# State products ahead of score sums, and weight conversion regrouped, in a fused recurrent-attention and two-stage MoE kernel

## The chip, the cores and the metric

One core of one Trainium2 chip runs the whole program. The metric is device time in microseconds (us) of one execution; the kernel before has a median of 840.31 us over 3 runs (839.7 to 840.45). Five engines work side by side, each through its own queue in program order, and wait for one another through semaphores: TensorE (PE, matmuls), VectorE (DVE), ScalarE (ACT), GpSimd (POOL) and SyncE (SP, which here issues the DMAs).

## The reference

```python
for t in range(S):                          # B, H, S, D = 4, 8, 768, 48
    kt, vt, rt = (k[:, :, t], v[:, :, t], r[:, :, t])
    cur = np.einsum('bhd,bhe->bhde', u[None] * kt, vt)
    y[:, :, t] = np.einsum('bhd,bhde->bhe', rt, state + cur)
    state = w[None, :, :, None] * state + np.einsum('bhd,bhe->bhde', kt, vt)
...
h = x @ w_in                                # 3072 tokens, 384 -> 2048; weights in float64
g = np.maximum(h, 0.0) + alpha * np.minimum(h, 0.0)
x = (g @ w_out).astype(np.float32)          # 2048 -> 384
...
logits = x @ w_gate                         # 8 experts, 384 tokens each, best logits first
h = np.maximum(x[mask] @ w1[e], 0.0)        # 384 -> 1024
out[mask] = h @ w2[e]                       # 1024 -> 384
```

Three stages follow one another: a recurrence over 768 positions with a 48x48 state for each of 32 heads, a leaky-ReLU MLP over all 3072 tokens, and a routed MLP in which each token goes to one expert.

## The kernel before, in words

The recurrence is computed in chunks of 128 positions: 24 chunks, in the order chunk-major over 4 batch entries. `turn(i)` (L353) works on chunk i and finishes chunk i-1; it is a generator of four sections, and the loop at L1271 runs turns 0 to 24. Within a turn PE gets, in this order: the products of the scaled receptance with the stored state into y (L371, only from the second chunk of a batch entry on), four transposes of a later chunk's keys into pk (L339), the score sums of chunk i+1 (`sums`, L308: 16 tiny matmuls of prod with uw into the last eight columns of the tile kvc), the state products kv of chunk i (L390, into the first columns of the same tile kvc, not in the last four turns that have a chunk), the products of V with the masked scores AT of chunk i-1 into y (L397), and the scores pA of chunk i (L424). DVE copies pA into AT by predicate at the start of the next turn (L366), scales the receptance (RT, L331), copies the sums to cs (L318) and adds kv to the state (Sn, L402). ACT writes the scaled diagonals of AT (L378, L405), copies pk to KT (L345) and y to ysb (L410). POOL scales keys (L324), decays the state (SW, L382) and multiplies RT by KT into prod (L351), which the sums of the next turn read. SP loads the chunks and stores ysb.

Between the sections of a turn runs a second generator, the weight preparation (`load_weights`, L462). The MLP multiplies in pairs of a high and a low part, so each of 32 pieces of its weights (16 of `w_in`, 16 of `w_out`, 128x384 each, in float64) is loaded three pieces ahead and converted in five steps (`weight_split`, L438). Steps 1 to 4 each have one DVE instruction (L449, L451, L453 into ti; L456 into tf), step 1 also the load of a later piece and mk on ACT (L446); step 5 is the cast of the high part on ACT (L459) and the subtraction for the low part on POOL (L460). `PACE` = 4 of these steps are taken in each turn from turn 2 on; after the loop a piece that has been begun is finished, and four warm-up matmuls follow (L1278 to L1280). That makes 19 pieces in this stage.

Then `mlp` (L575) takes the tokens in groups of 512, five of them, and two of 256. It splits the group's x into xh and xl (L512, L513), and for each of 16 steps f it does nine matmuls of layer 1 into ph (L656), reads ph twice on ACT (nt L660, gt L661), combines the two on DVE (gt, L669), casts to gh on ACT (L677) and subtracts for gl on DVE (L680). Layer 2 of step f (12 matmuls, L605) is issued two steps later. Each step also takes `rate` steps of a side generator (L678): in group 0 five steps of the weight preparation (13 pieces remain), in groups 1 and 2 the gate columns (L517), which read the gate table wgb. That table is loaded when group 1 begins (L624), into a pool opened where the pool of mk and tf was closed. Groups 3 and 4 have early logits there. The constants for routing, `route_consts` (L116), among them two zeroed tables ohr of 128x3072 bf16, are made on POOL and DVE right after the first x is split (L593).

Of the kernel before, what the change touches and what calls it, by code (L numbers as in the profile page):

```python
# [8 lines left out]
F32 = mybir.dt.float32  # L9
# [13 lines left out]
NTT = NT // P  # L23
# [4 lines left out]
GMAX = max(GROUPS)  # L28
WCG = 3
WO = DM + E  # L30
PACE = 4
BITS = (5, 5, 5, 5, 4, 4, 4)
STEPS = 4
TH = 32
# [25 lines left out]
def cut(g, n):  # L60
    for _ in range(n):
        if next(g, "end") == "end":
            return
        yield
# [21 lines left out]
class Kernel:  # L86
# [29 lines left out]
    def route_consts(self):  # L116
        nc, cp = self.nc, self.cp
        v, g = nc.vector, nc.gpsimd
        self.tri = cp.tile([P, P], BF, name="tri")
        v.tensor_scalar(self.tri, self.jp, 0.0, -1.0, op0=ALU.is_le, op1=ALU.mult)  # L120
        self.onesb = cp.tile([P, P], BF, name="onesb")
        g.memset(self.onesb, 1.0)
        self.ones48 = cp.tile([P, 2 * NTT], F32, name="ones48")
        g.memset(self.ones48, 1.0)
        io = cp.tile([P, P], F32, name="io")
        g.iota(io, pattern=[[1, P]], base=0, channel_multiplier=0, allow_small_or_imprecise_dtypes=True)
        self.io = io
        ii = cp.tile([P, NSL + TH], I32, name="ii")
        g.iota(ii[:, :NSL], pattern=[[1, NSL]], base=BASE32, channel_multiplier=0)
        g.iota(ii[:, NSL:], pattern=[[1, TH]], base=0, channel_multiplier=0)  # L130
        self.iob, self.ioa = ii[:, :NSL], ii[:, NSL:]
        self.io1 = cp.tile([P, TH], F32, name="io1")
        v.tensor_scalar(self.io1, io[:, :TH], 1.0, None, op0=ALU.add)
        self.pcol = cp.tile([P, 1], F32, name="pcol")
        g.iota(self.pcol, pattern=[[0, 1]], base=0, channel_multiplier=1, allow_small_or_imprecise_dtypes=True)
        self.ohr = []
        for i in range(2):
            t = self.rp.tile([P, NTT, 4, 32], BF, name=f"ohr{i}")
            g.memset(t, 0.0)
            self.ohr.append(t)  # L140
        S = self.S = self.ps.tile([P, 512], F32, name="S")
        self.kap, self.act, self.sel = S[:, 0:24], S[:, 24:48], S[:, 48:56]
        self.bad, self.esum, self.tau, self.u = S[:, 56:57], S[:, 57:58], S[:, 58:59], S[:, 64:88]
        self.xi, self.bi5, self.ai5 = (S[:, 96 + 24 * i:120 + 24 * i].bitcast(I32) for i in range(3))
        self.iot = S[:, 168:192]
        v.memset(S[:, 56:58], 0.0)
        v.memset(self.act, 1.0)
        v.tensor_copy(self.iot, io[:, :NTT])
# [156 lines left out]
            t = self.raw[n, i % NRAW[n]]  # L305
            self.nc.sync.dma_start(t.rearrange("p j t -> p (j t)") if n == "r" else t, src[c, b])

    def sums(self, i):  # L308
        if i >= NCH:
            return  # L310
        cc, prod = self.kvc[:, 4 * D:], self.prod.pop(i)
        for j in range(4):
            for c in range(2):
                o = slice(64 * c, 64 * c + 64)
                self.nc.tensor.matmul(cc[o, 2 * j:2 * j + 2], prod[:, j, o], self.uw[:, j, :], start=True, stop=True,
                                      skip_group_check=True)
        cs = self.cs[i] = self.wk.tile([P, H], F32, name="cs")
        self.nc.vector.tensor_copy(cs, cc)  # L318

    def scale_k(self, i, g=None):  # L320
        if i >= NCH:
# [31 lines left out]
    def turn(self, i):  # L353
# [26 lines left out]
        self.scale_r(i + LOOK)  # L380
        if prev and pc < NCB - 1:
            g.tensor_mul(self.SW[pb], self.Sn[(i - 1) % 2], self.WC)  # L382
        yield
        self.sums(i + 1)
        kv = None
        if cur and c < NCB - 1:
            kv = self.kvc[:112, :4 * D].rearrange("p (j d) -> p j d", j=4)
            for j in range(4):
                for q, m in enumerate((64, D)):
                    nc.tensor.matmul(kv[64 * q:64 * q + m, j, :], KP[:, 2 * j + q, :m], head(V, 2 * j + q, D),  # L390
                                     start=True, stop=True, skip_group_check=True)
        if prev:
            Vp, ATp = self.raw["v", (i - 1) % NRAW["v"]], self.AT.pop(i - 1)
            for j in range(4):
                for q in range(2):
                    m = 112 - 64 if q else 64
                    nc.tensor.matmul(y[64 * q:64 * q + m, j, :], head(Vp, 2 * j + q, m), ATp[:, q, j, :],  # L397
                                     start=(pc == 0), stop=True, skip_group_check=True)
        if kv is not None:
            for q in range(2):  # L400
                o = slice(64 * q, 64 * q + D)
                v.tensor_add(self.Sn[i % 2][o, :, o], kv[o], self.SW[b][o, :, o])  # L402
        if cur:
            for h in range(1, H, 2):
                nc.scalar.mul(AT[:, 1, h // 2, :], self.ident, cs[:, h:h + 1])  # L405
# [169 lines left out]
    def mlp(self, ctx):  # L575
# [11 lines left out]
        c0 = ExitStack()  # L587
        self.stg = self.pool(c0, "stg2", 2)
        side = self.wl
        rate = 5  # L590
        todo = []
        drain(self.split_x(0))
        self.route_consts()  # L593
        acc = pend = None

        def layer2(gi, f, gh, gl, tiles=None):
# [22 lines left out]
        for gi, T in enumerate(GROUPS):  # L619
# [23 lines left out]
            xh, xl = self.x  # L643
            nx = self.split_x(gi + 1) if gi < late else iter(())
            for f in range(NF):
                if f == 4 and gi < late:
                    self.fetch_x(gi + 1)
                if f > 9:
# [10 lines left out]
                gt = self.gp.tile([P, GMAX], F32, name="gt" if gi < late else "gh", bufs=2 if gi < late else 3)  # L659
                nc.scalar.activation(nt[:, :T], ph[:, :T], AF.Relu, scale=-1.0)  # L660
                nc.scalar.activation(gt[:, :T], ph[:, :T], AF.Relu)  # L661
                if len(todo) == (LAG if gi < late else LAG + 1):
                    j = todo.pop(0)
                    if j[0] < late:
                        assert self.split_done > NF + j[1]
                        layer2(*j)
                    else:
                        self.late_gate(lg, j)
# [580 lines left out]
def kernel(ctx, tc, *args):  # L1249
# [5 lines left out]
    with ExitStack() as c2:  # L1255
        K.pa = c2.enter_context(tc.tile_pool(name="pa", bufs=1, space=PSUM))
        K.rw = ctx.enter_context(tc.tile_pool(name="rw", bufs=4, reuse_waits="tile"))
        wl = K.wl = K.load_weights(WAHEAD)
        K.att_setup(c2)
        v = tc.nc.vector  # L1260
        for i in range(LOOK + 1):
            K.scale_k(i, None if i else v)
        for i in range(LOOK):
            K.scale_r(i)
            K.turn_k(i)
            K.keep_k(i)
            K.product(i, None if i else v)
        K.sums(0)
        for i in range(EARLYC, AHEAD):
            K.load_chunk(i)  # L1270
        for i in range(NCH + 1):  # L1271
            merge((K.turn(i), 1), (cut(wl, PACE) if i > 1 else None, 1))
            K.load_chunk(i + AHEAD)
            if 17 <= i < 20:
                K.fetch_x(0, (i - 17,))
            if i == 3:
                tc.nc.sync.dma_start(K.al, K.alpha.rearrange("(f p) -> p f", p=P))
        while K.splitting:  # L1278
            next(wl)
        K.warm(4)  # L1280
    K.pa = None
    tc.nc.vector.tensor_scalar(K.al, K.al, -1.0, None, op0=ALU.mult)
    K.mlp_pools(ctx)
# [46 lines left out]
```

## Time and profile before

| | |
|---|---|
| median of 3 runs | 840.31 us |
| profiled execution | 834.65 us, its span 832.9 us |
| busy, share of the span | PE 94%, DVE 69%, ACT 49%, POOL 34% |
| granted TensorE clock, mean | 0.98 |
| chain that ended last | PE 69%, DVE 15%, issue 6%, ACT 4% |
| bytes moved | 81.39 MB, mean 98 GB/s |

The page divides the span into 40 slices of 20.8 us. The attention loop fills the first seven, group 0 of the MLP the next three and a half; from there to slice 26 PE is busy in nine tenths or more of each slice. Busy shares say where an engine has no time left, and the chain says which engine's work was waited for; a PE share under nine tenths in a slice is where PE itself waited. Times in the rows below are counted from the span's start.

### The profile page before, as it was taken

The page shows a single profiled execution, that of the slowest core. Times are in us where ns is not written, and L with a number is a line of the kernel's source. Part 1 is how long each engine was busy: PE and PEld are TensorE (multiplying, and loading weights), DVE is VectorE, ACT ScalarE, POOL GpSimd, SP SyncE. Part 2 cuts the span into 40 slices and gives each one's busy share as a digit, 9 for nine tenths or more (in the row PEclk, how much of TensorE's full clock was granted, in tenths as well). Part 3 has the DMA queues.
Part 4 walks back from the last instruction along what each step waited for, and adds up shares of the span by engine and source line. Part 5 has one row for each costly group of instructions (what it writes and reads, how often), then busy time and mean ns, then how long its engine had stood idle before and what let it go on. Part 6 is the DMA issues. An engine that isn't in the chain of part 4 may idle for free.

```text
span 832.9 us, 16734 instructions
## 1 busy us (share of the span) xinstructions
PE 785.5 (94%) x6147; PEld 717.9 (86%) x6147; DVE 576.9 (69%) x1536; ACT 406.7 (49%) x875; POOL 280.2 (34%) x269
## 2 busy tenths in 40 slices
PE   7888889899999999999999999996999999999996
PEld 6677778687899999999999999986899999999996
DVE  5688888878789989988988434565766666664121
ACT  2777778455544444444444445542443443444341
POOL 5676774421000000000000000003476666668661
PEclk8799999999999999999999999998899999999999
DMA  6577785241220020021020001006434633635400
GB/s 196 171 215 209 210 237 149 86 131 39 77 76 1 0 77 1 10 96 30 19 70 27 1 26 33 20 1 197 155 92 147 209 102 109 202 111 173 142 30 31
DMA packets 64585, 81.39 MB, mean 98 GB/s; under 512 B 8048, under 2 KB 55408, under 8 KB 64368
## 3 DMA queue, kind: packets, MB, share of 16 engines
q1 hardware_dynamic: 61008, 70.81, 27.5%
q0 software_dynamic: 3072, 9.44, 3.3%
q8 instruction: 50, 0.82, 0.4%
q14 instruction: 39, 0.32, 0.1%
q10 hardware_dynamic: 416, 0.00, 0.0%
HBM read 66.07 MB, written 14.16 MB: 96 GB/s over the span
## 4 chain that ended last, share of the span: by engine, by line
PE 69%; DVE 15%; issue 6%; ACT 4%; POOL 2%; DMA 1%; DVEq 0%; POOLq 0%; SPq 0%; ACTq 0%
PE m L605 21%; PE ph L656 19%; PE eph L1106 10%; PE o L1123 9%; PE cnt L796 2%; DVE AT L366 2%; DVE ti L451 2%; DVE ti L449 2%; PE y L397 2%; PE kvc L390 1%; DVE ti L453 1%; DVE tf L456 1%; PE pA L424 1%; DVE RT L331 1%; ACT nt L660 1%
## 5 line engine op out<-in xcount | busy, mean ns | idle before, releaser
L605 PE MATMUL m<-wbh,gl 128*128 128x384 f32 (+1 forms) x352 | 120.4, 342 | 5.6 <-DVE gl L680 5.6
L656 PE MATMUL ph<-xh,wah 128*128 128x512 f32 (+1 forms) x336 | 122.7, 365 | 2.0 <-ACT xh L512 1.8
L656 PE MATMUL ph<-xl,wah 128*128 128x512 f32 (+1 forms) x336 | 122.7, 365 | 0.4 <-DVE xl L513 0.4
L656 PE MATMUL ph<-xh,wal 128*128 128x512 f32 (+1 forms) x336 | 122.5, 365 | 0.0
L605 PE MATMUL m<-wbh,gh 128*128 128x384 f32 (+1 forms) x352 | 119.5, 339 | 0.0
L605 PE MATMUL m<-wbl,gh 128*128 128x384 f32 (+1 forms) x352 | 119.3, 339 | 0.0
L660 ACT ACTIVATE nt<-ph 128x512 f32<-128x512 f32 (+1 forms) x112 | 60.1, 536 | 112.7 <-PE ph L656 106.8
L746 POOL COPY L<-M 128x176 f32<-128x176 f32 (+1 forms) x2 | 0.7, 356 | 339.0 <-DVE M L611 318.0
L669 DVE SCALAR_TENSOR_TENSOR gt<-nt,al,gt 128x512 f32<-128x512 f32 (+1 forms) x96 | 67.8, 706 | 52.7 <-ACT gt L661 52.7
L677 ACT CAST gh<-gt 128x512 fp32r<-128x512 f32 (+1 forms) x96 | 56.4, 587 | 75.5 <-DVE gt L669 75.5
L1114 DVE SCALAR_TENSOR_TENSOR hl<-eph,hh 128x384 fp32r<-128x384 f32 x64 | 35.6, 557 | 77.4 <-ACT hh L1109 77.4
L1109 ACT ACTIVATE hh<-eph 128x384 fp32r<-128x384 f32 x64 | 31.4, 491 | 114.6 <-PE eph L1106 110.1
L605 PEld LDWEIGHTS m<-wbh,gl 128*128 128x128 f32 x352 | 66.1, 188 | 9.8 <-DVE gl L680 9.8
L527 DVE SCALAR_TENSOR_TENSOR junk<-wt,wgb 128x384 f32<-128x384 f32 x128 | 71.3, 557 | 3.9
L656 PEld LDWEIGHTS ph<-xh,wal 128*128 128x128 f32 x336 | 63.4, 189 | 10.9
L656 PEld LDWEIGHTS ph<-xh,wah 128*128 128x128 f32 x336 | 63.6, 189 | 10.3 <-ACT xh L512 2.0
L680 DVE TENSOR_TENSOR gl<-gt,gh 128x512 fp32r<-128x512 f32 (+1 forms) x96 | 61.7, 643 | 14.1 <-ACT gh L677 14.0
L656 PEld LDWEIGHTS ph<-xl,wah 128*128 128x128 f32 x336 | 63.5, 189 | 8.5 <-DVE xl L513 0.9
L1070 POOL TENSOR_TENSOR wal<-raw,wah 128x768 fp32r<-128x768 f32 x32 | 58.4, 1846 | 33.5 <-ACT wah L1069 32.0
L605 PEld LDWEIGHTS m<-wbh,gh 128*128 128x128 f32 x352 | 66.1, 188 | 3.8 <-ACT gh L677 0.3
L605 PEld LDWEIGHTS m<-wbl,gh 128*128 128x128 f32 x352 | 66.2, 188 | 3.3
L1070 POOL TENSOR_TENSOR wbl<-raw,wbh 128x768 fp32r<-128x768 f32 x32 | 58.6, 1847 | 29.8 <-ACT wbh L1069 29.8
(252 smaller groups left out, 1799.2 us busy)
## 6 DMA issues: line engine op xcount, KB each, us to landing
raw<-in_moe_w_dram SPq DMA_DIRECT2D x64, 384.0 KB, 3.9
raw<-in_moe_w_in_dram SPq DMA_DIRECT2D x16, 384.0 KB, 4.3
raw<-in_moe_w_out_dram SPq DMA_DIRECT2D x16, 384.0 KB, 3.2
raw_r<-in_rt_dram SPq DMA_DIRECT2D x24, 224.0 KB, 3.9
raw_k<-in_kc_dram SPq DMA_DIRECT2D x24, 192.0 KB, 3.7
raw_v<-in_vc_dram SPq DMA_DIRECT2D x24, 192.0 KB, 4.1
xd<-ysb SPq DMA_DIRECT2D x48, 96.0 KB, 2.4
md<-raw SPq DMA_DIRECT2D x22, 192.0 KB, 1.9
```

The lines of the kernel that those rows point to most:

```text
L527: v.scalar_tensor_tensor(junk, t, 1.0, self.wgb[:, e], op0=ALU.mult, op1=ALU.mult, accum_out=wc[:, f, e:e + 1])
L605: nc.tensor.matmul(acc[t][:, :N], a[:, o], self.wb[b][:, f, :N], start=(f == 0 and n == 0), stop=(f == NF - 1 and n == 2))
L656: nc.tensor.matmul(ph[:, :T], self.wa[a][:, k, fs], b[:, k, :T], start=(n == 0), stop=(n == 8))
L660: nc.scalar.activation(nt[:, :T], ph[:, :T], AF.Relu, scale=-1.0)
L669: v.scalar_tensor_tensor(gt[:, :T], nt[:, :T], self.al[:, f:f + 1], gt[:, :T], op0=ALU.mult, op1=ALU.add)
L677: nc.scalar.copy(h, g)
L680: v.tensor_sub(l, g, h.bitcast(F32))
L1070: self.nc.gpsimd.tensor_sub(to[1], d, to[0].bitcast(F32))
L1106: self.nc.tensor.matmul(ph, w1[a][:, k, f * P:(f + 1) * P], x[b][:, k], start=(n == 0), stop=(n == 8))
L1109: self.nc.scalar.activation(hh, ph, AF.Relu)
L1114: self.nc.vector.scalar_tensor_tensor(hl, ph, 0.0, hh.bitcast(F32), op0=ALU.max, op1=ALU.subtract)
L1123: self.nc.tensor.matmul(self.acc[q], h[a][:, o], w2[b][:, f], start=(f == 0 and n == 0), stop=(f == NS - 1 and n == 2))
```

## The change

In a turn the kv matmuls are now issued in the first section, directly behind the transposes, and the sums behind them; the copy to cs becomes `keep_sums` and is issued behind the additions to the state. `PACE` becomes a list for turns 0 to 21: 4 and 4, then 4, 3, 4, 3, 4 four times over, 80 steps in all, which is 16 pieces. The finishing loop and the four warm-up matmuls after the attention go. In group 0 of the MLP four preparation steps are taken at the old place, and one (cast and low part) directly behind nt and gt of the next step; 16 pieces are converted there, and the last one's fifth step is issued when group 1 begins. `route_consts` is called in group 4 at step 12, and it zeroes each ohr in four instructions written as 32-bit words.

```diff
--- before.py
+++ after.py
@@ -28,7 +28,7 @@
 GMAX = max(GROUPS)
 WCG = 3
 WO = DM + E
-PACE = 4
+PACE = (4, 4) + (4, 3, 4, 3, 4) * 4
 BITS = (5, 5, 5, 5, 4, 4, 4)
 STEPS = 4
 TH = 32
@@ -136,7 +136,8 @@
         self.ohr = []
         for i in range(2):
             t = self.rp.tile([P, NTT, 4, 32], BF, name=f"ohr{i}")
-            g.memset(t, 0.0)
+            for a in range(0, NTT, 6):
+                g.memset(t[:, a:a + 6].rearrange("p a b e -> p (a b e)").bitcast(F32), 0.0)
             self.ohr.append(t)
         S = self.S = self.ps.tile([P, 512], F32, name="S")
         self.kap, self.act, self.sel = S[:, 0:24], S[:, 24:48], S[:, 48:56]
@@ -305,17 +306,21 @@
             t = self.raw[n, i % NRAW[n]]
             self.nc.sync.dma_start(t.rearrange("p j t -> p (j t)") if n == "r" else t, src[c, b])
 
-    def sums(self, i):
-        if i >= NCH:
+    def sums(self, prod):
+        if prod is None:
             return
-        cc, prod = self.kvc[:, 4 * D:], self.prod.pop(i)
+        cc = self.kvc[:, 4 * D:]
         for j in range(4):
             for c in range(2):
                 o = slice(64 * c, 64 * c + 64)
                 self.nc.tensor.matmul(cc[o, 2 * j:2 * j + 2], prod[:, j, o], self.uw[:, j, :], start=True, stop=True,
                                       skip_group_check=True)
+
+    def keep_sums(self, i):
+        if i >= NCH:
+            return
         cs = self.cs[i] = self.wk.tile([P, H], F32, name="cs")
-        self.nc.vector.tensor_copy(cs, cc)
+        self.nc.vector.tensor_copy(cs, self.kvc[:, 4 * D:])
 
     def scale_k(self, i, g=None):
         if i >= NCH:
@@ -380,8 +385,6 @@
         self.scale_r(i + LOOK)
         if prev and pc < NCB - 1:
             g.tensor_mul(self.SW[pb], self.Sn[(i - 1) % 2], self.WC)
-        yield
-        self.sums(i + 1)
         kv = None
         if cur and c < NCB - 1:
             kv = self.kvc[:112, :4 * D].rearrange("p (j d) -> p j d", j=4)
@@ -389,6 +392,9 @@
                 for q, m in enumerate((64, D)):
                     nc.tensor.matmul(kv[64 * q:64 * q + m, j, :], KP[:, 2 * j + q, :m], head(V, 2 * j + q, D),
                                      start=True, stop=True, skip_group_check=True)
+        prod = self.prod.pop(i + 1, None)
+        self.sums(prod)
+        yield
         if prev:
             Vp, ATp = self.raw["v", (i - 1) % NRAW["v"]], self.AT.pop(i - 1)
             for j in range(4):
@@ -400,6 +406,7 @@
             for q in range(2):
                 o = slice(64 * q, 64 * q + D)
                 v.tensor_add(self.Sn[i % 2][o, :, o], kv[o], self.SW[b][o, :, o])
+        self.keep_sums(i + 1)
         if cur:
             for h in range(1, H, 2):
                 nc.scalar.mul(AT[:, 1, h // 2, :], self.ident, cs[:, h:h + 1])
@@ -587,10 +594,9 @@
         c0 = ExitStack()
         self.stg = self.pool(c0, "stg2", 2)
         side = self.wl
-        rate = 5
+        rate = 4
         todo = []
         drain(self.split_x(0))
-        self.route_consts()
         acc = pend = None
 
         def layer2(gi, f, gh, gl, tiles=None):
@@ -643,6 +649,8 @@
             xh, xl = self.x
             nx = self.split_x(gi + 1) if gi < late else iter(())
             for f in range(NF):
+                if (gi, f) == (late - 2, 12):
+                    self.route_consts()
                 if f == 4 and gi < late:
                     self.fetch_x(gi + 1)
                 if f > 9:
@@ -659,6 +667,8 @@
                 gt = self.gp.tile([P, GMAX], F32, name="gt" if gi < late else "gh", bufs=2 if gi < late else 3)
                 nc.scalar.activation(nt[:, :T], ph[:, :T], AF.Relu, scale=-1.0)
                 nc.scalar.activation(gt[:, :T], ph[:, :T], AF.Relu)
+                if gi == 0 and f:
+                    drain(cut(side, 1))
                 if len(todo) == (LAG if gi < late else LAG + 1):
                     j = todo.pop(0)
                     if j[0] < late:
@@ -1265,19 +1275,18 @@
             K.turn_k(i)
             K.keep_k(i)
             K.product(i, None if i else v)
-        K.sums(0)
+        K.sums(K.prod.pop(0))
+        K.keep_sums(0)
         for i in range(EARLYC, AHEAD):
             K.load_chunk(i)
         for i in range(NCH + 1):
-            merge((K.turn(i), 1), (cut(wl, PACE) if i > 1 else None, 1))
+            merge((K.turn(i), 1), (cut(wl, PACE[i]) if i < len(PACE) else None, 1))
             K.load_chunk(i + AHEAD)
             if 17 <= i < 20:
                 K.fetch_x(0, (i - 17,))
             if i == 3:
                 tc.nc.sync.dma_start(K.al, K.alpha.rearrange("(f p) -> p f", p=P))
-        while K.splitting:
-            next(wl)
-        K.warm(4)
+        assert not K.splitting
     K.pa = None
     tc.nc.vector.tensor_scalar(K.al, K.al, -1.0, None, op0=ALU.mult)
     K.mlp_pools(ctx)
```

## Rows read from the trace of the kernel before

**Rows 1.** Windows of the attention loop: us, busy by engine, granted clock, DMA share, GB/s

```profile
84.00:123.00 39.00, 33.67 (x550) 29.65 (x548) 32.02 (x68) 30.92 (x87) 29.17 (x29) 1.00 0.75 223
```

**Rows 2.** Waits, 20 to 140 us: who waited for whom, us in total, times, longest

```profile
PE kvc L390 <- DVE cs L318: 15.0, 19, 2.0
```

**Rows 3.** Timeline of PE, one turn: start, us, engine, line, op, operands, count [idle before]

```profile
90.62 0.61 PE L390 MATMUL kvc<-raw_v,raw_p 128*64 128x48 f32 x15 [0.61 <-DVE cs L318]
...
93.19 1.13 PE L371 MATMUL y<-RT,SW 112*112 112x128 f32 x8
...
94.69 0.63 PE L315 MATMUL kvc<-uw,prod 112*64 112x2 f32 x16
```

**Rows 4.** Timeline of DVE, the same turn

```profile
88.58 1.34 DVE L366 COPY_PREDICATED AT<-later,pA 128x512 f32<-128x512 int32 x2
...
91.41 0.72 DVE L402 TENSOR_TENSOR Sn<-kvc,SW 48x192 f32<-48x192 f32 x2 [0.84 <-PE kvc L390]
92.16 0.56 DVE L449 TENSOR_SCALAR ti<-raw 128x384 uint32<-128x384 uint32 x1
...
93.95 1.36 DVE L366 COPY_PREDICATED AT<-later,pA 128x512 f32<-128x512 int32 x2
```

**Rows 5.** Timeline of all engines, one step of MLP group 0

```profile
161.97 0.59 ACT L660 ACTIVATE nt<-ph 128x512 f32<-128x512 f32 x1
...
163.08 0.75 DVE L669 SCALAR_TENSOR_TENSOR gt<-nt,al,gt 128x512 f32<-128x512 f32 x1 [0.96 <-ACT gt L661]
...
166.10 0.69 DVE L680 TENSOR_TENSOR gl<-gt,gh 128x512 fp32r<-128x512 f32 x1
...
166.22 0.51 ACT L459 CAST wbh<-tf 128x384 fp32r<-128x384 f32 x1 [1.28 <-DVE tf L456]
...
166.64 0.59 ACT L660 ACTIVATE nt<-ph 128x512 f32<-128x512 f32 x1
```

**Rows 6.** Chain of waits at the end of group 0: start, us, what

```profile
217.11 2.10 PE ph L656 x9
219.21 2.09 PE m L605 x12
```

**Rows 7.** Timeline of all engines, from the last turn into the MLP

```profile
142.49 1.58 PE L397 MATMUL y<-AT,raw_v 128*64 128x128 f32 x16
...
144.10 0.58 ACT L410 COPY ysb<-y 112x512 f32<-112x512 f32 x1 [0.19 <-PE y L397]
...
145.88 0.51 ACT L459 CAST wbh<-tf 128x384 fp32r<-128x384 f32 x1 [0.73 <-DVE tf L456]
146.30 1.66 ACT L512 CAST xh<-xr 128x512 fp32r<-128x512 f32 x3
...
146.95 2.28 DVE L513 TENSOR_TENSOR xl<-xr,xh 128x512 fp32r<-128x512 f32 x3 [1.01 <-ACT xh L512]
...
146.97 0.73 PE L656 MATMUL ph<-xh,wah 128*128 128x512 f32 x1 [1.81 <-ACT xh L512]
...
148.12 5.24 POOL L139 MEMSET ohr<- 128x3072 bf16 x2
...
149.15 4.30 DVE L120 TENSOR_SCALAR tri<-jp 128x128 bf16<-128x128 int32 x1
...
151.12 0.39 PE L656 MATMUL ph<-xh,wah 128*128 128x512 f32 x1
...
157.54 0.44 PE L605 MATMUL m<-wbh,gl 128*128 128x384 f32 x1 [1.60 <-DVE gl L680]
```

**Rows 8.** Windows, the first layer-1 matmuls

```profile
147.00:150.50 3.50, 3.12 (x7) 2.14 (x8) 3.50 (x5) 0.96 (x2) 3.50 (x8) 0.51 0.61 215
```

**Rows 9.** Timeline of all engines, end of the weight conversion

```profile
215.07 1.01 POOL L460 TENSOR_TENSOR wbl<-tf,wbh 128x384 fp32r<-128x384 f32 x1 [4.18 <-ACT wbh L459]
...
216.10 0.33 SPq L624 DMA_DIRECT2D wgb<-in_moe_w_gate_dram  x1
```

**Rows 10.** Windows, the transfer of the gate table

```profile
221.00:222.00 1.00, 1.00 (x6) 0.87 (x5) 0.60 (x1) 0.36 (x1) 0.00 (x0) 1.00 0.38 160
```

## The prediction

> **What bounds the kernel now.** I read the page's busy shares first, then the chain that ended last, the waits of each stage, and the timelines of one turn or one step. TensorE (PE) is busy 94% of the span, so only stretches where PE stands still can give time. Two are touched by the change.
>
> In the attention loop (to about 144 us) PE has 33.67 us of work in 39 us at full granted clock [rows 1]. One wait makes up nearly all the rest: the state products (kv, L390) stand behind the score sums in PE's queue and wait until VectorE (DVE) has copied the sums to cs: 15.0 us over 19 turns [rows 2]. The reader sees it in one turn: kv at 90.62 after 0.61 us idle, although kv needs nothing of the sums; the two only share the tile kvc [rows 3]. DVE in turn idles 0.84 us until kv is there [rows 4]. Each engine waits once for the other in every turn.
>
> In MLP group 0 PE is not the bound either. A step there takes 4.67 us (nt at 161.97, next nt at 166.64) [rows 5], while a step's matmuls take 2.10 + 2.09 = 4.19 us where nothing waits [rows 6]. The period is a closed loop over two engines: nt and gt on ScalarE (ACT), gt and four conversion steps on DVE, then the piece's cast, which sits on ACT ahead of the next nt and stands 1.28 us waiting for tf [rows 5].
>
> Durations below are from the profiled execution: span 832.9, time 834.65 us. The timed runs have a median of 840.31; I take the difference worked out in the one off the other, so 5.7 us between them stays.
>
> **1. Attention: kv ahead of the sums.** No instruction goes; eight instruction groups change place. From kv at 90.62 to the end of the sums (94.69 + 0.63) PE runs 4.70 us without a gap [rows 3]; that is the new turn if nothing else is late. What is late next? DVE: from 88.58 to 93.95 is 5.37 us, 0.84 of it idle, with three conversion instructions at 0.60 (92.16 to 93.95) [rows 4]. So 4.53 - 1.80 = 2.73 us are fixed. The new pacing gives 18 generator steps in five turns, four in five of them a DVE instruction: 2.88 x 0.60 = 1.73. DVE then needs 4.46 us, under 4.70, and its idle time goes too, because kv and sums are done when it comes to Sn and cs. A turn with four conversions needs 5.13, so DVE falls behind by 0.4 and recovers in the next. PE tolerates that: between pA and the y products that read AT it has 1.50 us (L371 and the transposes, 93.19 to 94.69), kv 0.5 and sums 0.6, against 1.25 for the two predicated copies, about 1.3 us to spare [rows 3, 4].
>
> The sums now wait for prod on GpSimd (POOL) at a point some 0.5 us later than before, so that wait can't grow. The cs copy comes behind Sn, 0.7 us later on DVE; its reader, the first scaling of the next turn on ACT, is queued behind ysb and so isn't due by then. Turns before the fifth have no L371, so PE needs only 3.7 there and DVE's 4.46 sets them: three turns x 0.75 = 2.2 us of the 15.0 stay. I take **-13** us. Bounds: -16, all waits and a little half-clock time, and -1, if the transfers can't be served faster than now (their share is 0.75 in this stretch [rows 1]; one in 4.70 us would be 0.84). I side with -13, since a share of 0.84 is still under full.
>
> Sixteen pieces instead of nineteen fit in this loop, starting two turns earlier. DVE and ACT mostly idle in turns 0 and 1, so I cost the early start at nothing (0 to +1 if ACT's order delays the predicated copies).
>
> **2. Into the MLP.** Before, PE ends its last y at 144.07 (142.49 + 1.58); the first layer-1 matmul starts at 146.97, 2.90 us later, because ACT holds xh behind the cast of a nineteenth piece (145.88) that waits for DVE [rows 7]. With no piece left, ACT does ysb (0.58) and the first xh (1.66/3 = 0.55): 1.2 us. **-1.7.** The warm matmuls lay inside the wait, so removing them is free by itself. The first nine matmuls took 4.15 us (146.97 to 151.12) [rows 7] at a granted clock of 0.51, half speed, after 1.81 us of idle [rows 7, 8]. At full speed they need 2.10, and the three xl at about 0.75 each stretch that to 2.8. Whether the clock falls again with a gap of 1.2 us and no warm matmuls is open: 0 or -1.35; the gap is shorter, so I take **-1.3**.
>
> **3. Group 0.** All sixteen pieces of the second weight are now converted here, one per step. The cast moves behind nt and gt of the next step, so ACT no longer waits for tf. DVE's own step is gt to the end of gl, 163.08 to 166.79 = 3.7 us [rows 5], under PE's 4.19, so PE sets the period. A piece must be ready sooner: cast and low part end about 1.1 + 0.5 + 1.0 = 2.6 us after the layer-1 product of the next step, and the layer-2 product that reads them starts 4.19 us after it; 1.6 us to spare. Only the first one is tight: the low part of piece 16 comes some 1.5 us after PE could use it. That replaces the present wait for gl at 157.54 (1.60 us), caused by DVE standing in tri until 153.45 [rows 7]: **-0.2**. From that matmul to group 1's first product is 221.30 - 157.54 = 63.8 us [rows 6, 7]; new: 10 matmuls of 0.174 and 13 steps of 4.19, 56.2. **-7.5** (bounds -8 and 0). The three xl of the next group add 0.7 to 1.0 us each on DVE in steps 10 to 12; gl has about 3.4 us to spare, so that is hidden, and steps 13 to 15 repay half a microsecond each.
>
> **4. What that makes late: wgb.** The 1.5 MB gate table is loaded into the memory of the conversion's buffers: its issue at 216.10 follows the last low part (215.07 + 1.01), and the transfers run until about 221.4 [rows 9, 10], ahead of group 1. Now the last piece ends in group 1: its cast waits for tf, about 0.5 us after the next layer-1 product could be evicted, then 1.0 on POOL, then 5.5 us of transfer. The table lands about 7.5 to 8.5 us after the end of group 1's first product; DVE wants it at 2.5 and stands in the first junk instruction with gl queued behind it. gl then ends near 11, where PE wants it at 8.7. **+2** (0 to +5, the latter if the wait isn't absorbed by the next steps).
>
> **5. Routing tables.** The POOL memsets (5.24 us for two) and the small DVE instructions go to step 12 of group 4. There DVE has neither conversions nor early logits, only gt, gl and one xl in 4.19 us. Even if it were held as long as tri was (4.30 us [rows 7]), gl has more than that to spare: 0 (0 to +2). Eight memsets of a quarter the elements each can only shorten the hold.
>
> Sum: -13 - 1.7 - 1.3 - 0.2 - 7.5 + 2 = **-21.7**. The profiled execution comes to 813.0, the median to **818.6 us**.
>
> **Rivals.**
> *A, the loop finds another pace.* kv no longer waits, but y does, on predicated copies that DVE, ACT or a late chunk delays. For it: DVE would be 95% busy, and transfers at 0.84 share land later. Against it: 1.3 us of tolerance. The turn would stop near 5.05: 20 x 0.35 = 7 us lost, 825.6.
> *B, POOL and DVE collide in group 0.* The low part (1.01 us [rows 9]) ran in DVE's idle time before gt; now it can fall beside gt, gl or xl. tri took 4.30 us while POOL's memsets ran [rows 7], so one can hold the other. DVE's step would be 3.7 + 1.0 = 4.7, the old period: 13 x 0.5 = 6.8 us, 825.4. Against it: POOL's part starts after gt has begun, and two steps of slack. [...]
> *C, it doesn't do what it says.* kv waits now for a copy of other columns of its tile, so it may as well wait for Sn or cs of the turn before. Those end more than 2 us before kv comes, so the price would be nil; only if kv still found itself behind the copy would the 13 us stay: 831.6.
> *D, slower.* PE falls to half clock in the loop, as it did for 147 to 150.5 [rows 8]. A turn of 4.70 becomes up to 9.4, 4.7 more than forecast; from five such turns in addition on, 23 us, the kernel is slower: 842 and up. Against it: the loop at 0.86 busy was granted 1.00 throughout [rows 1], and it gets busier. The Trainium skill, "TensorE: Matmul & The Clock Gate", section "HAM oscillation — how this bites in real kernels", puts the fall down to idle gaps; the change takes gaps out.
>
> **How the numbers follow.** Forecast 0.70 (814 to 823 by itself), A 0.13, B 0.08, C 0.04, D 0.02, and 0.03 for more gain than forecast, where the early turns' half clock also goes. Range 812 to 827: it takes in A and B, and leaves out C, D and the outer ends. Faster by over 0.2% (what a measurement can tell here) is everything but D and a mishap: 0.96; the same 0.02; slower 0.02.
>
> **What would show it.** Step 1: the row of kv waiting for cs gone, turns of 4.7 to 4.8 us from the fifth on, the loop ending near 131. If y's loads wait for AT instead, it is A. Step 2: about 1.2 us from the last y to the first layer-1 product, granted clock near 1. Step 3: nt every 4.19 us in group 0, cast without a wait for tf; DVE's gt or gl at over 1 us would be B. Step 4: DVE idle on wgb in group 1, PE waiting some 2 us for one gl. Step 5: no PE wait in group 4. The prediction is wrong if the loop keeps over 5.0 us a turn, or if group 1 loses more than 5.

## The result, and the profile after

| | before | after |
|---|---|---|
| median | 840.07 us (839.7 to 840.45, 4 runs) | 818.09 us (817.3 to 819.96, 4 runs) |
| ratio of the medians | | 0.974 (95% interval 0.9723 to 0.976) |
| profiled execution, its span | 834.65, 832.9 us | 817.63, 815.9 us |
| busy: PE, DVE | 94%, 69% | 95%, 70% |
| chain that ended last: PE, DVE | 69%, 15% | 69%, 6% |

The change takes 22 us off; the forecast was 818.6 us. That the two agree so closely owes something to errors of opposite sign, and the two profiled executions differ by 17.0 us only. Cutting each span at the last `ysb` (end of the attention loop), at group 5's first nt and at the last hh of the experts (ACT's reading of an expert's first product) shows both:

| us | loop ends | loop end to group 5 | group 5 to last hh |
|---|---|---|---|
| before | 144.1 | 348.5 | 326.4 |
| after | 126.5 | 342.6 | 332.9 |
| difference | -17.6 | -5.9 | +6.5 |

The last column isn't the change: in a later execution of the kernel before, that stage took 333.5 us (at the end of the experiments). So the change itself is worth 23.5 us between these two profiles, where 21.7 were forecast.

**Attention loop.** Windows of after: us, busy by engine, granted clock, DMA share, GB/s; the second answers to [rows 1].

```profile
36.00:104.00 68.00, 67.97 (x1137) 60.80 (x1136) 64.17 (x135) 62.21 (x176) 57.68 (x56) 1.00 0.87 251
84.00:123.00 39.00, 38.52 (x601) 33.98 (x602) 32.16 (x66) 34.92 (x100) 27.14 (x26) 1.00 0.76 222
```

PE has 0.03 us of idle time left in 68 us. The transfers keep up at a DMA share of 0.87. Waits of PE in after, 15 to 131 us (us in total, times, longest), answering to [rows 2]:

```profile
PE pk L344 <- ACT KT L350: 3.0, 1, 3.0
PE ph L664 <- ACT xh L519: 1.2, 1, 1.2
PE kvc L316 <- POOL prod L356: 0.3, 1, 0.3
```

The row of kv waiting for cs is gone. One turn on PE (start, us, engine, line, op), answering to [rows 3]:

```profile
91.06 0.61 PE L393 MATMUL kvc<-raw_v,raw_p 128*64 128x48 f32 x15
...
91.53 0.56 PE L316 MATMUL kvc<-uw,prod 112*64 112x2 f32 x14
...
92.02 1.07 PE L403 MATMUL y<-AT,raw_v 128*64 128x128 f32 x15
...
95.60 0.61 PE L393 MATMUL kvc<-raw_v,raw_p 128*64 128x48 f32 x15
```

From kv to kv is 4.54 us. The sums begin while the last kv matmuls still run: the two together take 0.96 us (91.06 to 92.02), not 0.61 + 0.63. The same turn on DVE, answering to [rows 4]:

```profile
89.76 1.35 DVE L371 COPY_PREDICATED AT<-later,pA 128x512 f32<-128x512 int32 x2
...
92.28 0.72 DVE L408 TENSOR_TENSOR Sn<-kvc,SW 48x192 f32<-48x192 f32 x2
93.04 0.17 DVE L323 COPY cs<-kvc 128x8 f32<-128x8 f32 x1
...
94.30 1.36 DVE L371 COPY_PREDICATED AT<-later,pA 128x512 f32<-128x512 int32 x2
```

Sn now has no idle time before it. DVE is busy 64.17 of 68 us, so it stands close behind PE.

**Into the MLP.** All engines, answering to [rows 7]:

```profile
124.90 1.56 PE L403 MATMUL y<-AT,raw_v 128*64 128x128 f32 x16
...
126.50 0.58 ACT L417 COPY ysb<-y 112x512 f32<-112x512 f32 x1 [3.06 <-PE y L403]
126.98 1.66 ACT L519 CAST xh<-xr 128x512 fp32r<-128x512 f32 x3
...
127.65 0.50 PE L664 MATMUL ph<-xh,wah 128*128 128x512 f32 x1 [1.19 <-ACT xh L519]
...
130.40 0.39 PE L664 MATMUL ph<-xh,wah 128*128 128x512 f32 x1
...
135.42 0.44 PE L611 MATMUL m<-wbh,gh 128*128 128x384 f32 x1 [0.66 <-ACT wbh L466]
135.44 1.50 POOL L467 TENSOR_TENSOR wbl<-tf,wbh 128x384 fp32r<-128x384 f32 x1 [17.82 <-ACT wbh L466]
...
137.00 0.44 PE L611 MATMUL m<-wbl,gh 128*128 128x384 f32 x1 [1.14 <-POOL wbl L467]
...
137.28 0.34 PE L611 MATMUL m<-wbh,gl 128*128 128x384 f32 x1
```

```profile
128.00:131.00 3.00, 2.72 (x12) 2.11 (x12) 1.58 (x3) 1.04 (x3) 0.00 (x0) 1.00 0.66 194
```

The gap is 1.19 us where it was 2.90, and the first nine matmuls take 2.75 us (127.65 to 130.40) where they took 4.15; the granted clock is 1.00 from 128 to 131 us. Then layer 2 waits for the first piece twice: 0.66 us for its high part (wbh, the cast on ACT) and 1.14 us for its low part (wbl, the subtraction on POOL), which takes 1.50 us.

**Group 0.** One step, answering to [rows 5]:

```profile
162.41 0.60 ACT L668 ACTIVATE nt<-ph 128x512 f32<-128x512 f32 x1 [1.21 <-PE ph L664]
...
163.38 0.52 ACT L466 CAST wbh<-tf 128x384 fp32r<-128x384 f32 x1
163.53 0.75 DVE L679 SCALAR_TENSOR_TENSOR gt<-nt,al,gt 128x512 f32<-128x512 f32 x1 [0.49 <-ACT gt L669]
163.98 1.19 POOL L467 TENSOR_TENSOR wbl<-tf,wbh 128x384 fp32r<-128x384 f32 x1 [3.01 <-ACT wbh L466]
...
166.62 0.60 ACT L668 ACTIVATE nt<-ph 128x512 f32<-128x512 f32 x1 [1.21 <-PE ph L664]
```

The step is 4.21 us where it was 4.67 (nt to nt). The cast waits for nothing, and nt now waits for PE.

**The gate table in group 1.** The chain of waits from the last low part on (start, us, what), answering to [rows 6, 9, 10]:

```profile
196.71 1.02 POOL wbl L467
...
197.75 6.06 DMA wgb<-in_moe_w_gate_dram
...
203.91 0.58 DVE junk L534 x2
...
206.28 0.62 DVE gl L690
...
206.94 2.57 PE m L611 x10
209.50 3.08 PE ph L664 x9
```

And the windows behind it:

```profile
206.00:208.00 2.00, 1.06 (x6) 1.07 (x7) 2.00 (x6) 0.42 (x1) 0.00 (x0) 1.00 0.91 304
208.00:212.00 4.00, 4.00 (x14) 3.42 (x13) 3.86 (x12) 1.80 (x4) 0.00 (x0) 0.57 0.01 3
```

PE waits 2.21 us for gl, which is queued on DVE behind the junk instructions (the products for the gate columns, L534) that read the table. Then the granted clock is 0.57 on average for 4 us, so most of them at the lower of its two levels, 1.2 GHz: ten layer-2 matmuls take 2.57 us instead of 10 x 0.174 ([rows 6]: 2.09 us for 12), and nine of layer 1 take 3.08 instead of the 2.10 of [rows 6]. From group 1's first product to its end is 73.6 us, 4.1 more than before.

**Routing tables.** POOL reaches the instructions written in group 4 as soon as its last subtraction is done, since they depend on nothing:

```profile
198.38 2.93 POOL L140 MEMSET ohr<- 128x384 f32 x8
```

No wait of PE names them.

### The profile page after: what moved, and what is told of

Read it like the earlier page. It is cut to its first block, busy times and chain, and to the rows that moved or that the text cites. A ratio compares the mean times of both kernels' runs of the same rounds, so it can differ in the third digit from the quotient of the medians.

```text
span 815.9 us, 16696 instructions
## 1 busy us (share of the span) xinstructions
PE 778.5 (95%) x6139; PEld 715.5 (88%) x6139; DVE 570.6 (70%) x1536; ACT 405.6 (50%) x875; POOL 280.4 (34%) x275
## 4 chain that ended last, share of the span: by engine, by line
PE 69%; DVE 6%; issue 4%; POOL 2%; ACT 2%; another core or an unknown queue 1%; DMA 1%; POOLq 0%; ACTq 0%; DVEq 0%
PE m L611 24%; PE ph L664 22%; PE eph L1116 10%; PE o L1133 9%; PE cnt L806 2%; PE ept L1100 1%; DMA wgb<-in_moe_w_gate_dram 1%; DVE hl L1124 1%; DVE gh L679 1%; ACT nt L668 1%; POOL out_dram L1142 1%; POOL wbl L1080 1%; DVE G L801 1%; POOL wbl L467 0%
## 5 line engine op out<-in xcount | busy, mean ns | idle before, releaser
L534 DVE SCALAR_TENSOR_TENSOR junk<-wt,wgb 128x384 f32<-128x384 f32 x128 | 71.3, 557 | 8.9 <-DMA wgb<-in_moe_w_gate_dram 5.0
L1080 POOL TENSOR_TENSOR wbl<-raw,wbh 128x768 fp32r<-128x768 f32 x32 | 58.5, 1850 | 31.4 <-ACT wbh L1079 21.7
```

The costliest lines, as they stand in the source:

```text
L534: v.scalar_tensor_tensor(junk, t, 1.0, self.wgb[:, e], op0=ALU.mult, op1=ALU.mult, accum_out=wc[:, f, e:e + 1])
L1080: self.nc.gpsimd.tensor_sub(to[1], d, to[0].bitcast(F32))
```

## The experiments

Kernels marked (i) ran on one chip beside the kernel before at a median of 835.56 us (833.5 to 841.0, 17 runs), those marked (ii) on another at 847.57 (844.0 to 848.5, 9 runs), those marked (iii) on a third at 843.03 (841.4 to 848.3, 13 runs). Intervals of ratios are against the kernel before on the same chip.

**The order of the turn alone (i).** The kernel before, with the sums behind kv and nothing else:

```diff
-        yield
-        self.sums(i + 1)
         kv = None
...
+        prod = self.prod.pop(i + 1, None)
+        self.sums(prod)
+        yield
         if prev:
...
+        self.keep_sums(i + 1)
```

> The kernel before with one part of the change alone: state products ahead of the score sums, the copy to cs behind the additions to the state. Pacing, finishing loop, casts and tables stay as before. Theory (the order gives most of what the loop gives): the wait of the state products for cs goes, a turn falls from 5.4 to about 4.7 us, the loop ends 12 to 15 us earlier; 826 us (825 to 829). Rival (DVE sets the loop unless it gets fewer conversions): with 3.2 conversion instructions a turn DVE needs 2.73 + 3.2 x 0.60 = 4.65 us and jitter, turns stay near 5.0; 833 us.

Measured 816.7 us (815.28 to 817.35), ratio 0.9758 (0.9723 to 0.9793), 18.9 us under the kernel before. Of the 9 us under what I expected, half is the chip, where the kernel before has 835.6 and not 840.3 us, and half the loop, which gained 17.9 us and not 12 to 15. Windows, and ACT at the end of the loop:

```profile
36.00:104.00 68.00, 67.47 (x1124) 60.18 (x1120) 65.16 (x138) 60.83 (x172) 58.19 (x58) 1.00 0.89 251
```

```profile
126.23 0.59 ACT L416 COPY ysb<-y 112x512 f32<-112x512 f32 x1 [0.19 <-PE y L402]
...
128.01 0.51 ACT L465 CAST wbh<-tf 128x384 fp32r<-128x384 f32 x1 [0.73 <-DVE tf L462]
128.43 1.66 ACT L518 CAST xh<-xr 128x512 fp32r<-128x512 f32 x3
```

The last ysb comes at 126.23, as in after (126.50): the order alone gives the whole gain of the loop, and converting 19 pieces there instead of 16 costs it nothing. The late xh, behind a nineteenth cast, is still there, and group 0 keeps its pace.

**Everything but the order (i).** After, with the old order of the turn (the same edit the other way round).

> The changed kernel with the order of a turn put back: score sums ahead of the state products. Pacing, casts behind evictions and late tables as in the changed kernel. Theory: the wait for cs comes back, some 0.6 us and more in twenty turns; 832 us (830 to 834). Rival (the new pacing gives a good part of the loop's gain, DVE has less to do before cs): turns of about 5.0; 826 us.

Measured 832.9 us (831.73 to 834.58), ratio 0.9959 (0.9938 to 0.998). The wait is back (waits, 15 to 140 us), and the last ysb comes at 145.9:

```profile
PE kvc L391 <- DVE cs L319: 13.8, 20, 1.5
```

From the loop's end to group 5 it takes 344.3 us, 4.2 under the kernel before, but its loop ends 1.8 us later than there. With the run above this makes the order nearly all of the result on this chip (18.9 us alone), and the rest of the change a few us (2.7 alone).

**The cast at its old place (i).**

```diff
-        rate = 4
+        rate = 5
...
-                if gi == 0 and f:
-                    drain(cut(side, 1))
```

> The changed kernel with the cast and low part in group 0 at the old place (five preparation steps behind gh, none behind the evictions). Theory: nt waits for the cast and the cast for tf again, 4.67 us a step instead of 4.19 in 16 steps, 7.7 us; the last piece then ends before group 1, so the gate table comes some 2 us earlier and takes 1 to 4 back; 822 to 825 us. Rival (group 0 gains from nothing else than the freed start, casts hide anyway): 818 us.

Measured 822.75 us (821.73 to 824.68), ratio 0.9837 (0.9801 to 0.9873). ACT and POOL in one step, then PE's waits of 125 to 240 us:

```profile
161.44 0.51 ACT L466 CAST wbh<-tf 128x384 fp32r<-128x384 f32 x1 [1.27 <-DVE tf L463]
...
161.86 0.59 ACT L668 ACTIVATE nt<-ph 128x512 f32<-128x512 f32 x1
...
162.03 1.01 POOL L467 TENSOR_TENSOR wbl<-tf,wbh 128x384 fp32r<-128x384 f32 x1 [3.66 <-ACT wbh L466]
```

```profile
PE m L611 <- DVE gl L688: 5.3, 1, 5.3
PE m L611 <- POOL wbl L467: 5.0, 16, 0.6
```

The cast waits again and nt stands behind it; the steps are back at 4.67 us (nt at 129.2, 133.9, 138.5). From the loop's end to group 5 takes 354.8 us, 12.2 more than in after (the changed kernel did not run on this chip, but on three sets of runs this stage took 342.6 to 343.0); beside the early table on the same chip (next run) the time is 14.3 us longer. The chain of [rows 5] was therefore what set the step, and the cast's place what took it away; PE meets it here as 16 waits for the low part, 5.0 us in all. The table's wait does not shrink, as I had thought, but grows to 5.3 us, since the last piece still ends in group 1.

**The gate table early (i).** After, with the table in memory of its own and loaded in step 8 of group 0:

```diff
+        self.wgb = self.pool(cb, "bg", 1).tile([P, E, DM], F32, name="wgb")
...
+                if (gi, f) == (0, 8):
+                    nc.sync.dma_start(self.wgb, ...
```

> The changed kernel, the gate table in memory of its own and its load issued in step 8 of group 0 instead of at the start of group 1. Theory: DVE's 5.0 us wait for the table goes, with it PE's 2.4 us wait for gl and the half-clock stretch behind it (3.3 us at half, 1.65 us): 4 us less, 814 us. Rival (the clock stretch comes at another place anyway): 2.4 us less, 815.7. Rival (the load in group 0 delays weight pieces): 818 or more.

Measured 808.41 us (806.21 to 810.51), ratio 0.9656 (0.9619 to 0.9693), below the 814 that I expected in part because this chip's stage of the experts is the short one (326.2 us). PE's waits of 125 to 240 us name gl no more:

```profile
PE ph L665 <- ACT xh L519: 1.2, 1, 1.2
PE m L612 <- POOL wbl L467: 1.1, 1, 1.1
PE m L612 <- ACT wbh L466: 0.6, 1, 0.6
```

Group 1, first nt to group 2's first, takes 66.8 us where after takes 70.75 and before 67.28: the late table costs 4.0 us. From the loop's end to group 5 only 2.4 of them show, because here the clock fell behind the two waits for the first piece (0.60 in 140 to 143 us), which it did not in after.

**The changed kernel again, on two chips.** (ii):

> The changed kernel once more, for a direct comparison with the partial kernels. Theory (the 6 us that its profiled execution took longer than the kernel before in the expert stage, 332.9 against 326.4 us from group 5 on, were the execution's and not the change's): that stage near 326 us here and 812 us in all. Rival (the change itself lengthens the expert stage): 332 us there and 818 us.

818.32 us (817.45 to 821.1), ratio 0.9675 (0.9648 to 0.9703). The 326 us that I expected from group 5 on did not come: the stage took 334.0. (iii):

> The changed kernel beside the two others on the same chip. Theory: 0.967 to 0.975 of the kernel before, with the stage from group 5 on as long as in the kernel before on this chip, within 1 us. Rival (the change lengthens that stage): 6 us longer than there.

818.38 us (817.24 to 820.61), ratio 0.9691 (0.9641 to 0.974). Here the stage took 334.2 us, and 333.5 in the kernel before on the same chip (last run): the change does not lengthen it. The changed kernel hardly moves in its three sets of runs; the kernel before does (840.1, 847.6 and 843.0 us), so the ratio goes from 0.967 to 0.974.

**The tables at their old place (ii).** Made right after the first x is split, with the two long memsets.

> The changed kernel with the routing tables made where the kernel before makes them, with memsets of bf16 as there. Theory: POOL and DVE are freer at the end of the loop now, but POOL's memsets (5.2 us) come ahead of the low part of piece 16, and DVE stands in tri behind them: 0 to 2 us more than the changed kernel. Rival (the move is worth its own 1.3 us and the first gl): 2 to 4 us more.

Measured 821.69 us (820.07 to 822.98), 3.4 more than the changed kernel beside it; ratio 0.9701 (0.9675 to 0.9727), whose interval overlaps with that of the changed kernel. POOL and DVE:

```profile
118.20 5.24 POOL L139 MEMSET ohr<- 128x3072 bf16 x2
```

```profile
129.44 0.22 DVE L120 TENSOR_SCALAR tri<-jp 128x128 bf16<-128x128 int32 x1
```

With no piece left for POOL at the loop's end the memsets run inside the loop, and tri, which took 4.30 us beside them before [rows 7], takes 0.22. So the old place adds no wait of PE, once the attention stage ends without a piece: PE's waits of 125 to 240 us are those of the changed kernel. Of the 3.4 us, the profiled executions put 1.5 on one step of group 0 at a granted clock of 0.71, which kernels with the new place had too (below), and 1.2 on the stage of the experts. That the move itself is worth anything isn't shown.

**The sums twice (ii).** After, with the 16 tiny matmuls of the sums issued twice per turn: PE gets more work, and DVE none.

```diff
         self.sums(prod)
+        self.sums(prod)
         yield
```

> The changed kernel with the score sums issued twice in each turn, with the same result: 16 tiny matmuls more on PE, some 0.45 us. Theory (PE sets the loop): 23 x 0.45 = 10 us more than the changed kernel. Rival (DVE or a transfer sets it and PE has slack): 0 to 4 us more.

Measured 830.94 us (827.68 to 838.48), 12.6 more than after beside it, ratio 0.9797 (0.9766 to 0.9829). The turn is 5.01 us. Its profiled execution (838.48) is the slowest of its runs, and its windows show why:

```profile
30.00:40.00 10.00, 10.00 (x124) 9.10 (x124) 5.52 (x13) 5.40 (x16) 5.34 (x5) 0.50 0.52 154
...
50.00:60.00 10.00, 10.00 (x188) 9.08 (x184) 7.85 (x17) 7.01 (x20) 6.34 (x6) 1.00 0.68 204
```

PE sets the pace: the turn is 0.47 us longer, and that is what 16 more of these matmuls take (30 in 1.03 us, where after has 14 in 0.56). And for some 30 us (20 to 50) the clock was at half while PE was busy 29.69 of them, which is what rival D feared, without the extent that it would need.

**RT twice (iii).** After, with the scaling of the receptance done twice on DVE: 0.6 to 0.7 us more there, nothing on PE.

```diff
         self.nc.vector.tensor_mul(RT, self.raw["r", i % NRAW["r"]], self.TR)
+        self.nc.vector.tensor_mul(RT, self.raw["r", i % NRAW["r"]], self.TR)
```

> The changed kernel with the scaling of the receptance issued twice in each turn on DVE, with the same result: 0.6 us more DVE work a turn. Theory (PE sets the loop at 4.54 us a turn, DVE stands close behind with some 4.4): DVE sets it then with 5.0, 0.45 x 20 = 9 us more than the changed kernel. Rival (DVE has the whole of its 0.6 us to spare): 0 to 3 us more.

Measured 831.03 us (829.12 to 832.04), 12.65 more than after beside it, ratio 0.983 (0.9781 to 0.9879).

```profile
36.00:104.00 68.00, 64.92 (x1020) 55.93 (x1019) 65.39 (x135) 55.10 (x156) 51.37 (x51) 1.00 0.77 221
```

Now PE idles 3 us of 68, DVE is the bound, and the turn is 5.0 us on average (4.54 to 5.52): of 0.6 to 0.7 us some 0.46 is paid. So DVE had only about 0.1 to 0.2 us to spare in a turn; its idle time in after, 3.83 us in the 15 turns of 68 us, says 0.26. The loop ends 10.3 us later; most of the rest goes in the first steps of group 0, with a granted clock of 0.84 from 136 to 150 us (0.60 from 137.8 to 142, behind the same gap of 1.19 us that has 1.00 behind it in after).

**Early table and a seventeenth piece in the loop (ii).** The version that the runs point to: the early table, and the pace

```diff
-PACE = (4, 4) + (4, 3, 4, 3, 4) * 4
+PACE = (4,) * 21 + (1,)
```

> The kernel with the early gate table, and with 17 pieces instead of 16 in the attention loop (four steps in turns 0 to 20, one in turn 21). Theory (PE, not DVE, sets the loop, so 3.2 conversion instructions a turn are as good as 2.9; the first layer-2 product then finds its weights): the 1.8 us that PE waits there for cast and low part go, 806.5 us, 2 less than with the early table alone. Rival (DVE is as near its limit as PE): the loop takes 0.1 to 0.2 us a turn more, 2 to 4 us, and nothing is won: 808 to 811 us.

Measured 813.01 us (811.18 to 813.57), ratio 0.9595 (0.957 to 0.962), 5.3 us under after on the same chip. Its ratio is the lowest of all, but the changed kernel's own goes from 0.967 to 0.974 by chip. The first layer-2 matmuls find their piece ready, and one wait of 0.4 us is left where two made 1.8 (PE's waits, 125 to 240 us):

```profile
PE m L612 <- DVE gl L691: 0.4, 1, 0.4
```

The loop ends at 126.03 all the same, and loop end to group 5 is 336.9 us, 5.7 under after and 3.2 under the early table alone. The absolute time that I had expected missed, as the stage of the experts took 334.5 us here and 326.2 in the run it was reckoned from.

**The kernel before again (iii).**

> The kernel before once more with a profile, because its profiled execution (834.65 us) was 5.7 us shorter than its timed runs. Theory (the difference lies in the expert stage and goes with the chip or the execution): the stage from group 5 on takes 332 us here against 326.4 in the profile shown, and the loop ends near 144 us as there. Rival (the first turns of the loop at half clock make the difference): the loop ends later than 146 us and the expert stage takes 326.

Measured 843.47 us (840.96 to 847.86), ratio 0.9999 (0.9967 to 1.0031). Windows of the experts (first to last hh), first the profiled execution that the forecast was made from, then this one:

```profile
588.50:819.00 230.50, 226.93 (x1915) 217.75 (x1914) 126.22 (x398) 96.31 (x170) 152.10 (x124) 1.00 0.40 133
```

```profile
588.90:825.50 236.60, 227.84 (x1913) 217.85 (x1913) 126.63 (x398) 96.46 (x170) 152.24 (x124) 1.00 0.39 129
```

The same instructions, the same clock, and 6.1 us more, of which 0.9 is busy time of PE and the rest its idle time. All four kernels profiled on (i) had the short stage (326.2 to 326.3 us from group 5 on), all seven on (ii) and (iii) and the profiled execution of after the long one (332.9 to 335.1). So in these runs it goes with the chip, whatever the kernel. What in a chip makes it isn't settled: the chain of waits puts 1% of the span on "another core or an unknown queue" here and in after, and nothing in the profiled before, but nothing either in the early table with the seventeenth piece, which had the long stage too. It has nothing to do with the change, but a profiled before with the short stage against an after with the long one hides 6.5 us of a gain.

## Why the prediction was right, and by how much its steps were off

| step | forecast | measured |
|---|---|---|
| 1. loop | -13 | -17.6 |
| 2. gap, first nine matmuls | -1.7, -1.3 | -1.7, -1.4 |
| 3. first layer-2 matmuls | -0.2 | +0.5 |
| 3. group 0 steps | -7.5 | -7.35 |
| 4. gate table | +2 | +4.1 |
| 5. routing tables | 0 | 0 |
| sum | -21.7 | -23.5 |

**Step 1, the loop.** The mechanism was right, and the order alone gives it all, but its size was not: 17.6 us lie beyond the outer bound of 16. Cut at the sixth start of kv (47.80 us before, 40.68 after) and at the twentieth (123.44 and 104.68), the loop gains 7.1 us up to the first cut, 11.6 between the two, and loses 1.2 behind. Two terms were off.

The steady turn came to 4.54 us, not 4.70: I added the durations of kv and sums as if one began where the other ended, but issued together they overlap (0.96 us for both). In the 14 turns between the cuts the forecast comes to 75.64 - 14 x 4.70 = 9.8 us, so 1.8 of the excess lie here.

In the first turns the forecast leaves 3.2 us, and 7.1 came. I had kept back 2.2 us for turns in which DVE would be late; a turn without L371 at the upper clock takes 3.69 us (kv at 32.39 and 36.08), PE's time as forecast, so DVE wasn't late there. The half clock shrank as well: from 10 to 40 us the mean granted clock was 0.72 before and is 0.83 in after. The forecast had named that, with a chance of 0.03. How much each of the two gave isn't shown.

In one thing the forecast was nearer than its numbers: DVE is the next bound, and RT twice puts it 0.1 to 0.2 us behind, near the 0.24 (4.70 - 4.46) that I reckoned. The DMA bound (-1) did not bite: the transfers were served at 0.87.

**Step 2** came as reckoned, the clock included: behind a gap of 1.19 us it was at its upper level, where one of 1.81 us [rows 7] stood ahead of half clock. The shorter gap doesn't make that certain: nine profiled executions with it have a granted clock of 1.00 behind it, but RT twice has 0.60 from 137.8 to 142 us.

**Step 3.** The group's step went to PE's own 4.2 us, and with the cast back at its old place to 4.67. The first layer-2 matmuls were 0.7 us worse than forecast, 0.5 of it because I took 1.01 us [rows 9] for a low part that then took 1.50: its start falls beside DVE's gt. That is the collision of rival B, and the trace shows who is held: gt keeps its 0.75 us and POOL takes 1.50 (1.19 in steady steps), so the DVE step of 4.7 us that the rival needed never came. The Trainium skill, "SBUF — State Buffer", section "Who interferes with whom", says that a VectorE instruction with two SBUF inputs contends with a GpSimd instruction that reads SBUF; the trace agrees with 1.50 and 1.19 us against 1.01. It doesn't cover tri's 4.30 us [rows 7], since tri reads one tile and POOL's memsets read none. In one respect the changed kernel was lucky: behind the two waits for the first piece (0.66 and 1.14 us) five other kernels lost 1.5 us in a step at a granted clock of 0.71, and none of its own three profiled executions did.

**Step 4 is the term that was mis-sized to the bad side:** +4.1 us, within its range of 0 to +5. The table landed where I had put it and gl was late by 2.2 us, but I had no term for what follows a wait of 2.2 us on PE: the half clock that [rows 8] show after a similar one, here another 1.8 us ((2.57 - 1.74) + (3.08 - 2.10)). The early table removes it all.

**Step 5.** No cost, as forecast, but the work wasn't done where I put it: POOL made the tables in group 1, directly behind its last subtraction. An instruction that depends on nothing runs when its engine's queue reaches it, and the place in the code only says behind what.

**Rivals.** A (another pace): the loop did find DVE and the transfers close behind, but at 4.54 us, not 5.05. B: present, too small. C: the row of kv waiting for cs is gone. D: half clock showed for 30 us in one execution of a kernel with more matmuls, not in the changed one beyond the early turns that have it before as well. The granted 1.00 of [rows 1] that spoke against D is that of 84 to 123 us; the first turns stood at 0.72 already (10 to 40 us). Two small slips of the working change no chance: the two predicated copies take 1.34 us in [rows 4], not 1.25, and 13 x 0.5 for B are 6.5 us, not 6.8.

That the forecast came out 0.5 us from the median has a share of luck. The change was worth 23.5 us between profiled executions, not 21.7: the loop gave 4.6 more than its term, the gate table and the first layer-2 matmuls took back 2.8. And the profiled before that I started from had the short stage of the experts, while I let the 5.7 us to the median of its runs stand unexplained; that those runs had the long stage would explain them, but none of them has a profile.

## What to carry to other kernels

Where two engines each wait once for the other in every turn, look for two products that share a tile but not a value: issuing the one that needs nothing first took 17.9 us of 144 here, by order alone. Price an engine's new turn from its start-to-start times and not from the sum of its rows, since adjacent groups of matmuls overlap. For a transfer into reused memory count the wait of PE and the clock behind it, and before you subtract one profiled execution from another, compare a stage that the change doesn't touch, and take both on one chip.

## What was not expected of the hardware

- The clock stayed at half for about 30 us while PE was busy 97% to 100% of each ten (the sums twice, 20 to 50 us), behind an idle stretch of 2.7 us, and rose again with PE as busy as before. In the changed kernel, behind an idle stretch of 3.0 us at the same place, it has 0.68 from 20 to 36 us and 1.00 from there.
- The same wait need not have the same clock behind it. Behind the gap of 1.19 us into the MLP it was 1.00 in nine profiled executions and 0.60 in one (RT twice). Eight profiled executions have the waits of 0.7 and 1.1 us for the first piece; in five (the old order, the early table, the tables at their old place, the sums twice, RT twice) the step behind them took 5.8 us at a granted clock of 0.71, in the three of the changed kernel 4.3 us at 1.00. No run here shows what decides it.
- The experts' stage takes 326 us in every kernel profiled on one chip and 333 to 335 on two others, with the same instructions at full clock.
- One small DVE instruction (tri) takes 4.30 us beside two long memsets on POOL, ending 0.1 us behind them [rows 7], and 0.22 when they don't overlap; beside gt it is POOL's subtraction that is stretched, 1.01 to 1.50 us.
